# A two-layer MLP kernel: w2 loaded in four transfers of nine row tiles in place of six of six

## The chip, the cores and the metric

The kernel runs on one core of one Trainium2 chip. The metric is device time in microseconds (us) of one execution. The program uses one core, so there is no second die to compare. The kernel before takes 290.91 us (median of 3 runs, 290.85 to 291.09). A profile's span is about 1.8 us shorter than the time of the same run.

## The reference

```python
B, S, D, F = 1, 2048, 576, 4608          # all bf16
h   = einsum("bsd,df->bsf", x, w1) + b1
h   = relu(h) ** 2
out = einsum("bsf,fd->bsd", h, w2) + b2
```

w2 is 4608 x 576 in bf16: 36 row tiles of 128 rows, 5.31 MB, nearly half of the 11.36 MB that the profile counts as read from HBM (that count is the sum of all loads but the three blocks of x that are transposed on the way).

## The kernel before

The 2048 rows of x are taken in four blocks of 512. The first layer (`a_full`, `a_rows`) makes the 36 tiles of h for a block, and the second layer (`phase_t` for 128 of the 576 output columns, transposed; `phase_b` for the other 448) reduces over those 36 tiles. The order is: first layer of blocks 0 and 1, second layer of 0 and 1, then the same for blocks 2 and 3. So w2 is not needed until two first layers are done.

The w2 load and its place among the loads on the SyncE queue (SP), with cuts:

```python
    w2_sb = wpool.tile([P, NFT, D], BF16, name="w2_sb")         # NFT = 36
    w2_view = w2.rearrange("(ft p) d -> p ft d", p=P)
    W2CH = 6

    def load_w2(c):
        keep(nc.sync.dma_start(out=w2_sb[:, c * W2CH:(c + 1) * W2CH, :],
                               in_=w2_view[:, c * W2CH:(c + 1) * W2CH, :]))
    # ... cut ...
    load_xT(1)                                  # second x block, transposed by DMA
    for (j0, j1) in [(12, 14), (14, 16)]:       # the last parts of w1
        load_w1(nc.sync, 0, j0, j1)
        load_w1(nc.sync, 1, j0, j1)
    keep(nc.sync.dma_start(out=b2_bc[:], in_=b2.partition_broadcast(P)))
    for c in (0, 3, 1, 4, 2, 5):
        load_w2(c)
    load_xT(2)

    alloc_hT(0)
    a_full(0, "k_outer")
    a_rows(0, 12, 1)
    alloc_hT(1)
    load_xT(3)
    a_rows(1)
    a_full(1, "rows_first")
    phase_t(0, hTs[0])                          # the first reader of w2
    # ... cut ...
```

`phase_t` reads w2 in the order in which the first layer makes the tiles of h: 4, 20, 5, 21, 6, 22, ... 19, 35, then 0 to 3. That is why the chunks are loaded from both halves alternately.

```python
    ft_order = list(range(G))                   # G = 4, NJ = 16
    for j in range(NJ):
        ft_order += [G + j, G + NJ + j]
    t_order = ft_order[G:] + ft_order[:G]

    def phase_t(sb, hT):
        pt = ps_o.tile([P, SB], FP32, name="pt", tag="po")
        for i, ft in enumerate(t_order):
            keep(nc.tensor.matmul(pt[:], lhsT=w2_sb[:, ft, DM:D], rhs=hT[:, ft, :],
                                  start=(i == 0), stop=(i == NFT - 1)))
        # ... cut: bias, transposed store ...
```

## Time and profile before

| What | Before | Where it is read |
|---|---|---|
| time, median of the first 3 runs | 290.91 us | the runs |
| span, TensorE busy | 289.4 us, 285.2 us (99%) | the page, part 1 |
| granted TensorE clock | 1.0 | the list of cores |
| w2: issued, landed | 28.0 to 39.4 us on the queue; the last one, issued at 37.3 us, within 10.3 us | timeline of SP, the tile's own view |
| first reader of w2 | 75.7 us | the tile's own view |

The page of the kernel before. PE is TensorE; "busy" is in us with the share of the span; the DMA row is the busy share in tenths for 40 slices of 7.2 us, and the row under it what was moved in each slice. The last line is one kind of transfer: how many, the size of one, and the median time from issue to landing.

```profile
span 289.4 us, 4699 instructions
PE 285.2 (99%) x2032; PEld 138.9 (48%) x2032; DVE 78.5 (27%) x176; ACT 96.7 (33%) x154; POOL 2.3 (1%) x10
...
DMA  7999999400001100000000000000000110000000
GB/s 196 222 248 179 320 386 218 85 0 2 0 18 34 38 16 18 16 16 18 16 16 2 1 2 0 2 0 2 0 2 0 36 39 16 16 17 32 19 16 18
...
w_sb<-in_w_dram SPq DMA_DIRECT2D x6, 864.0 KB, 9.9
```

TensorE is busy throughout, while the DMA engines are nearly idle after the eighth slice. The view of waits, for TensorE (PE) alone, shows how little it stands still (us in total, times, longest):

```profile
PE wps L63 <- PEq L344: 0.8, 1, 0.8
PE pn L227 <- DMA w1n<-in_w_dram: 0.2, 1, 0.2
```

Neither of the two waits is on w2. The timeline of the SP queue (start, duration, operation) shows where w2 is issued: behind w1 and b2, ahead of the third x block.

```profile
26.99 0.94 SPq L304 DMA_DIRECT2D b_bc<-in_b_dram  x1
27.97 11.43 SPq L134 DMA_DIRECT2D w_sb<-in_w_dram  x6
39.44 7.88 SPq L126 DMA_TRANSPOSE xTw<-in_x_dram  x1
```

The stages are seen best in the chain of waits (start, duration, what). Line L270 is `phase_t`, L289 `phase_b`, L291 the addition of b2 to the last output:

```profile
76.09 15.54 PE pt L270 x72
91.63 54.48 PE po L289 x288
...
286.40 0.29 DVE o_sb L291
```

The view by windows (window, its length, then busy us of PE, PEld, DVE, ACT, POOL with the number of instructions, the granted clock, the DMA share and GB/s) shows the rate at which w2 arrives:

```profile
12.00:75.70 63.70, 63.70 (x577) 28.57 (x574) 29.85 (x70) 42.42 (x68) 0.00 (x0) 1.00 0.72 173
36.00:40.00 4.00, 4.00 (x42) 1.76 (x38) 2.23 (x6) 2.65 (x5) 0.00 (x0) 1.00 1.09 389
```

TensorE is busy 63.70 of 63.70 us up to the first use of w2, and the DMA engines move 389 GB/s while w2 is in flight. (The DMA share can come out above 1, as here.)

The slack is read from the view of the tile of w2: the first weight load that reads it (count, then min/median/max duration in ns, first and last start), its six transfers, and the time from issue to landing.

```profile
L270 PEld LDWEIGHTS <-w_sb x144: 98/98/98, 75.7 to 231.2; 128*128 128x128 bf16 x144
L134 SPq DMA_DIRECT2D w_sb<-in_w_dram x6: 1526/1873/2223, 28.0 to 37.3; - x6
DMA to landing us min/median/max: 8.3/9.9/10.3
```

The last transfer has landed by 37.3 + 10.3 = 47.6 us at the latest, about 28 us before 75.7 us.

### The profile page before, as it was taken

The numbers are of one execution on the slowest core, as the hardware profiler recorded it, in microseconds if no ns is written. First come the engines' busy times: TensorE is split into PE (matmuls) and PEld (weight loads), VectorE is DVE, ScalarE is ACT, GpSimd is POOL, SyncE is SP. The second block draws the span as 40 slices with busy tenths as digits, with TensorE's granted clock in tenths as the row PEclk, the third lists the DMA queues.
The fourth block names the chain that finished last, engine by engine and source line by source line (L and its number), as shares of the span: only waits on it lengthen the run. The fifth ranks groups of instructions, "written<-read, shape, count | busy, mean of one in ns | idle before, by whom it ended". The sixth has DMA issues, their size and how long they took to land.

```text
span 289.4 us, 4699 instructions
## 1 busy us (share of the span) xinstructions
PE 285.2 (99%) x2032; PEld 138.9 (48%) x2032; DVE 78.5 (27%) x176; ACT 96.7 (33%) x154; POOL 2.3 (1%) x10
## 2 busy tenths in 40 slices
PE   8999999999999999999999999999999999999995
PEld 4544444444444555555544444444444455555554
DVE  1644544444500200000025444444440001100001
ACT  3666666666500000000027666666770000000000
POOL 3000000000000000000000000000000000000000
PEclk9999999999999999999999999999999999999999
DMA  7999999400001100000000000000000110000000
GB/s 196 222 248 179 320 386 218 85 0 2 0 18 34 38 16 18 16 16 18 16 16 2 1 2 0 2 0 2 0 2 0 36 39 16 16 17 32 19 16 18
DMA packets 31637, 16.52 MB, mean 57 GB/s; under 512 B 15732, under 2 KB 31616, under 8 KB 31616
## 3 DMA queue, kind: packets, MB, share of 16 engines
q1 hardware_dynamic: 31264, 15.91, 22.1%
q8 instruction: 16, 0.26, 0.4%
q10 hardware_dynamic: 288, 0.30, 0.3%
q14 instruction: 5, 0.04, 0.0%
q0 software_dynamic: 64, 0.01, 0.0%
HBM read 11.36 MB, written 2.36 MB: 47 GB/s over the span
## 4 chain that ended last, share of the span: by engine, by line
PE 97%; DMA 1%; SPq 0%; DVE 0%; issue 0%
PE ph L188 42%; PE po L289 38%; PE pt L270 11%; PE pn L209 4%; DMA w1n<-in_w_dram 1%; PE pn L227 1%; PE ph L190 1%; PE pn L203 1%; SPq L75 0%; SPq L72 0%; DVE o_sb L291 0%; PE tb L149 0%; PE b1T_ps L166 0%; PE pn L205 0%
## 5 line engine op out<-in xcount | busy, mean ns | idle before, releaser
L188 PE MATMUL ph<-xTw,w_h 64*128 64x512 bf16 x576 | 124.6, 376 | 0.0
L190 PE MATMUL ph<-xTw,w_h 64*128 64x512 bf16 x576 | 124.6, 376 | 0.0
L289 PE MATMUL po<-w_sb,hT 128*128 128x448 bf16 (+2 forms) x612 | 109.4, 341 | 0.0
L176 ACT ACTIVATE r<-ph,b1T 128x512 bf16<-128x512 f32 x128 | 81.1, 685 | 41.6 <-PE ph L190 41.6
L188 PEld LDWEIGHTS <-w_h 64*128 64x128 bf16 x576 | 54.1, 94 | 68.3
L289 PEld LDWEIGHTS <-hT 128*128 128x128 bf16 x612 | 58.5, 98 | 51.0
L177 DVE TENSOR_TENSOR hT<-r 128x512 bf16<-128x512 bf16 x144 | 61.2, 425 | 75.9 <-ACT r L176 75.7
L190 PEld LDWEIGHTS <-w_h 64*128 64x128 bf16 x576 | 54.1, 94 | 0.0
L291 DVE TENSOR_TENSOR o_sb<-po,b_bc 128x448 bf16<-128x448 f32 (+2 forms) x17 | 10.2, 597 | 125.8 <-PE po L289 125.8
L270 PE MATMUL pt<-hT,w_sb 128*128 128x512 bf16 x144 | 31.4, 379 | 0.0
L176 ACT ACTIVATE r<-pn,b1T 128x512 bf16<-128x512 f32 x16 | 10.3, 688 | 61.0 <-PE pn L205 59.6
L270 PEld LDWEIGHTS <-w_sb 128*128 128x128 bf16 x144 | 14.1, 98 | 17.0
L273 ACT ACTIVATE oT<-pt,b2T 128x512 bf16<-128x512 f32 x4 | 2.7, 687 | 28.3 <-PE pt L270 28.3
L209 PE MATMUL pn<-xTw,w1n 128*128 128x512 bf16 x48 | 10.9, 379 | 0.0
L209 PEld LDWEIGHTS <-w1n 128*128 128x128 bf16 x48 | 4.5, 98 | 6.0 <-issue 0.8
L227 PE MATMUL pn<-xTw,w1n 128*128 128x256 bf16 x32 | 4.2, 273 | 0.4 <-DMA w1n<-in_w_dram 0.2
L63 PE MATMUL wps<-const-bfloat16-1.0 128*128 128x512 bf16 (+1 forms) x7 | 2.8, 581 | 0.8 <-PEq L344 0.8
L227 PEld LDWEIGHTS <-w1n 128*128 128x128 bf16 x32 | 2.9, 98 | 1.2 <-DMA w1n<-in_w_dram 0.9
L119 DVE COPY xTw<-xTw 64x2048 bf16<-64x2048 bf16 x4 | 2.8, 689 | 0.2
L120 DVE COPY xTw<-xTw 64x2048 bf16<-64x2048 bf16 x4 | 2.7, 687 | 0.1
L156 DVE COPY xTw<-tb 128x256 bf16<-128x256 bf16 x4 | 1.1, 292 | 6.2 <-PE tb L149 6.2
L203 PE MATMUL pn<-xTw,w1n 64*128 64x512 bf16 x8 | 2.4, 379 | 0.0
(23 smaller groups left out, 13.8 us busy)
## 6 DMA issues: line engine op xcount, KB each, us to landing
w_sb<-in_w_dram SPq DMA_DIRECT2D x6, 864.0 KB, 9.9
w_h<-in_w_dram SPq DMA_DIRECT2D x14, 288.0 KB, 7.2
out_dram<-o_sb SPq DMA_DIRECT2D x15, 112.0 KB, 1.7
w_h<-in_w_dram SPq DMA_DIRECT2D x4, 144.0 KB, 3.6
w1n<-in_w_dram SPq DMA_DIRECT2D x4, 128.0 KB, 3.6
out_dram<-ot SPq DMA_DIRECT2D x4, 128.0 KB, 2.0
x_sb<-in_x_dram ACTq DMA_DIRECT2D x2, 144.0 KB, 2.9
x_sb<-in_x_dram SPq DMA_DIRECT2D x2, 144.0 KB, 3.3
```

The source lines that it names most:

```text
L63: keep(nc.tensor.matmul(wps[:, 0:n], lhsT=ones[:, 0:P], rhs=ones[:, 0:n], start=True, stop=True))
L119: keep(nc.vector.tensor_copy(out=xT[0:H, SPC:SPC + 4, :], in_=xT[H:P, E3:E3 + 4, :]))
L176: keep(nc.scalar.activation(out=r[:], in_=bank[:], func=ACT.Relu, bias=b1T[:, ft:ft + 1], scale=1.0))
L177: keep(nc.vector.tensor_tensor(out=hTs[sb][:, ft, :], in0=r[:], in1=r[:], op=ALU.mult))
L188: keep(nc.tensor.matmul(bx[:], lhsT=w1_h[0:H, LO_C[i], jc], rhs=xT[0:H, LO_W[i], :], start=(i == 0), stop=(i == NC - 1)))
L190: keep(nc.tensor.matmul(by[:], lhsT=w1_h[H:P, UP_C[i], jc], rhs=xT[H:P, UP_W[i], :], start=(i == 0), stop=(i == NC - 1)))
L203: keep(nc.tensor.matmul(banks[2 * i][:], lhsT=w1n8[0:H, i, :], rhs=xT[0:H, SPC, :], start=start, stop=stop, skip_group_check=order == "k_o ...
L209: keep(nc.tensor.matmul(banks[g][:], lhsT=w1n[:, k, g * P:(g + 1) * P], rhs=xT[:, O + k, :], start=start, stop=stop))
L227: keep(nc.tensor.matmul(banks[g][:, hc], lhsT=w1n[:, k, g * P:(g + 1) * P], rhs=xT[:, O + k, hc], start=(h == 0 and k == 0), stop=False, s ...
L270: keep(nc.tensor.matmul(pt[:], lhsT=w2_sb[:, ft, DM:D], rhs=hT[:, ft, :], start=(i == 0), stop=(i == NFT - 1)))
L289: keep(nc.tensor.matmul(po[:, 0:d1 - d0], lhsT=hT[:, ft, jj * P:(jj + 1) * P], rhs=w2_sb[:, ft, d0:d1], start=(i == 0), stop=(i == NFT - 1)))
L291: keep(nc.vector.tensor_tensor(out=o_sb[:, d0:d1], in0=po[:, 0:d1 - d0], in1=b2_bc[:, d0:d1], op=ALU.add))
```

## The change

Fewer, larger transfers for w2, on the idea that each transfer has a fixed cost: four of 1,296 KB in place of six of 864 KB. The order still alternates between the halves of w2.

```diff
-    W2CH = 6
+    W2CH = 9
...
-    for c in (0, 3, 1, 4, 2, 5):
+    for c in (0, 2, 1, 3):
         load_w2(c)
```

## The prediction

> **What bounds the kernel now.** TensorE. The page gives PE busy 285.2 us of a 289.4 us span (99%), granted clock 1.0 (list of cores). The waits view finds only two waits of PE: 0.8 us before the warm-up matmuls and 0.2 us for a w1 tile. The window table gives PE 63.70 of 63.70 us between 12.0 and 75.7 us, 16.30 of 16.30 between 75.7 and 92.0, and no gap over 0.04 us up to 286.4 us. The chain of waits is 97% PE; the rest is its start (x and w1 landing) and its tail (last addition 0.29 us, last store about 1.5 us).
>
> **What the change does.** The same 5.31 MB of w2 (6 x 864 KB) goes out as 4 transfers of 1,296 KB on the same queue, still bringing both halves (tiles 0-8 and 18-26) first. The order listing shows the same rows of PE, ACT, DVE and POOL. Only semaphore lanes rotate by two, so later stores wait for other, long finished transfers, and TensorE waits for w2 four times instead of six.
>
> **Cost.** Before, the six issues took 1.5 to 2.2 us each on the SP queue (11.43 us in all, from 28.0 to 39.4), each landing 8.3 to 10.3 us after its issue. At 32 to 46 us the core moved 342 to 392 GB/s, so the stretch is bound by bytes, which don't change. The Trainium skill (DMA: Bandwidth & Descriptors, Anatomy of one DMA) gives a fixed cost of about 2 us per transfer, which would make two fewer worth at most 4 us; I don't grant that, since six transfers overlap and the bytes already flow at that rate. Estimates: issues of about 2.3 to 3.3 us, 10 to 12 us in all; landing 10 to 15 us after issue; w2 complete at 46 to 50 us, against at most 37.3 + 10.3 = 47.6 us before. The next transfer, the transpose of the third x block, starts within 1.5 us of its former 39.4 us.
>
> **How much is on the critical path: none.** The first reader of w2 is the weight load of the transposed tail phase at 75.7 us: about 28 us of slack. The first layer of blocks 0 and 1 runs in between, and needs only w1 and x. The w1 transfers and the second x block are issued before w2 (until 27 us) and keep their times. The third and fourth x blocks, issued behind w2 (39 to 52 us; traffic over by 54 us), are read only from about 91.6 us on. PE runs at full density throughout, so freed DMA time can't speed it.
>
> **Predicted time:** 290.9 us, 290.3 to 291.6 us 8 times in 10. Faster by over 2%: 1%; within 2%: 98%; slower by over 2%: 1%.
>
> **What would show each step.** Right: PE busy within 0.3 us of 285.2; phases at 75.7, 91.6, 146.1 and 216 us unmoved within 0.3 us; no wait of PE for w2 in the waits view; four w2 issues of 1,296 KB, median issue and landing 1.3 to 1.5 times as long, total issue 10 to 12 us, same GB/s at 32 to 46 us. Wrong on bytes-bound: w2 done over 3 us earlier. Wrong on slack: idle time of PE before 91.6 us beyond what it had, or a shifted start of the tail phase.
>
> **What would make it wrong.** Longer w2 bursts disturbing the last w1 or second x block landings (those queue ahead, so I doubt it); the lane rotation making a late store wait for a slow transfer (all are spaced by 6 us and land in 2); a granted clock under 1.0; or a chip-to-chip difference of a few tenths of a microsecond, which most of my range is for.

## The result, and the profile after

The changed kernel takes 291.16 us (median of 4 runs, 290.94 to 291.46), the kernel before on the same chip 291.00 us (median of 4, 290.85 to 291.09). The ratio is 1.0007 with a 95% interval of 0.999 to 1.0024: the same. Here and below a ratio is the mean time of one kernel's fast runs over that of the other's fast runs of the same rounds, so it is not quite the ratio of the medians.

The page after, the same lines:

```profile
span 289.6 us, 4693 instructions
PE 285.5 (99%) x2027; PEld 139.9 (48%) x2032; DVE 78.6 (27%) x176; ACT 96.7 (33%) x154; POOL 2.3 (1%) x10
...
DMA  7999999400001200000000000000000110000000
GB/s 198 221 245 188 308 389 212 92 0 2 0 14 25 52 16 18 16 16 18 16 16 2 1 2 0 2 0 2 0 2 0 36 38 16 16 16 19 33 16 18
...
w_sb<-in_w_dram SPq DMA_DIRECT2D x4, 1296.0 KB, 12.7
```

The waits of TensorE, the SP queue and the chain of waits after:

```profile
PE wps L63 <- PEq L344: 0.8, 1, 0.8
PE pn L209 <- issue: 0.3, 2, 0.2
PE tb L149 <- DMA x_sb<-in_x_dram: 0.2, 1, 0.2
```

```profile
26.91 0.82 SPq L304 DMA_DIRECT2D b_bc<-in_b_dram  x1
27.77 10.21 SPq L134 DMA_DIRECT2D w_sb<-in_w_dram  x4
38.03 9.78 SPq L126 DMA_TRANSPOSE xTw<-in_x_dram  x1
```

```profile
76.61 7.34 PE pt L270 x34
84.00 8.15 PE pt L270 x37
92.15 54.48 PE po L289 x288
...
286.92 0.29 DVE o_sb L291
```

The tile of w2 after:

```profile
L134 SPq DMA_DIRECT2D w_sb<-in_w_dram x4: 423/3064/3531, 27.8 to 34.7; - x4
DMA to landing us min/median/max: 9.2/12.7/13.5
```

And the same two windows after:

```profile
12.00:75.70 63.70, 63.54 (x578) 28.63 (x576) 29.87 (x70) 42.49 (x68) 0.00 (x0) 1.00 0.73 173
36.00:40.00 4.00, 4.00 (x40) 1.83 (x38) 2.54 (x6) 2.65 (x5) 0.00 (x0) 1.00 1.08 390
```

The reader should see four things. The transfers of w2 are fewer and each takes longer to land (12.7 us median in place of 9.9). The bytes flow at the same rate (390 and 389 GB/s). TensorE waits for w2 in neither kernel. And every stage of the second trace lies 0.52 us later (92.15 against 91.63, 286.92 against 286.40), while the span is only 0.2 us longer: something at the start cost half a microsecond, and something at the very end gave 0.3 us back. Both are settled below. (In the chain after, the first stage of L270 comes in two pieces because two matmul records are missing from that trace: 142 in place of 144. The 63.54 us of the first window is another such gap.)

### The profile page after: what moved, and what is told of

Its sections match the earlier page's. It is cut to its first block, busy times and chain, and to the rows that moved or that the text cites. A ratio compares the mean times of both kernels' runs of the same rounds, so it can differ in the third digit from the quotient of the medians.

```text
span 289.6 us, 4693 instructions
## 1 busy us (share of the span) xinstructions
PE 285.5 (99%) x2027; PEld 139.9 (48%) x2032; DVE 78.6 (27%) x176; ACT 96.7 (33%) x154; POOL 2.3 (1%) x10
## 4 chain that ended last, share of the span: by engine, by line
PE 98%; DMA 1%; issue 0%; DVE 0%
PE ph L188 42%; PE po L289 38%; PE pt L270 11%; PE pn L209 4%; PE pn L227 1%; DMA x_sb<-in_x_dram 1%; PE tb L149 1%; PE ph L190 1%; PE pn L203 1%; DVE o_sb L291 0%; PE b1T_ps L166 0%; PE pn L205 0%
## 5 line engine op out<-in xcount | busy, mean ns | idle before, releaser
L270 PE MATMUL pt<-hT,w_sb 128*128 128x512 bf16 x142 | 31.3, 379 | 0.1
L270 PEld LDWEIGHTS <-w_sb 128*128 128x128 bf16 x144 | 14.1, 98 | 17.0
L227 PE MATMUL pn<-xTw,w1n 128*128 128x256 bf16 x32 | 4.6, 295 | 0.0
L227 PEld LDWEIGHTS <-w1n 128*128 128x128 bf16 x32 | 3.3, 107 | 0.5
L149 PE MATMUL tb<-ident,x_sb 128*128 128x128 bf16 x20 | 2.4, 288 | 0.2 <-DMA x_sb<-in_x_dram 0.2
## 6 DMA issues: line engine op xcount, KB each, us to landing
w_sb<-in_w_dram SPq DMA_DIRECT2D x4, 1296.0 KB, 12.7
```

The source lines that it names most:

```text
L149: keep(nc.tensor.transpose(bank[:, slot, qc], xs[:, j, c0:c0 + P], ident[:]))
L227: keep(nc.tensor.matmul(banks[g][:, hc], lhsT=w1n[:, k, g * P:(g + 1) * P], rhs=xT[:, O + k, hc], start=(h == 0 and k == 0), stop=False, s ...
```

## The experiments

The theory: w2 is off the path, because its last byte lands about 28 us before its first reader; while it is in flight the bytes bind, not the number of transfers. The rivals: each transfer has a cost that shows (the 2 us that the prediction quotes from the Trainium skill); the slack is not there or the traffic disturbs other stages; and, for the 0.52 us, that the change itself moved the stages.

Kernels are compared only within the same rounds. All outputs are right.

| Kernel | w2 load | Time, median us | Before, median us | Ratio, 95% interval |
|---|---|---|---|---|
| mid6 | 6 x 6, held to about 59 us | 291.28 | 291.29 | 1.0009 (0.9994 to 1.0023) |
| mid9 | 4 x 9, held to about 59 us | 291.34 | 291.29 | 1.0003 (0.9986 to 1.002) |
| late6 | 6 x 6, held to about 74 us | 301.45 | 291.29 | 1.0354 (1.0338 to 1.0369) |
| late9 | 4 x 9, held to about 74 us | 303.06 | 291.29 | 1.041 (1.0395 to 1.0426) |
| two18 | 2 x 18, old place | 290.94 | 291.43 | 0.9989 (0.9976 to 1.0001) |
| many36 | 36 x 1, old place | 290.72 | 291.43 | 0.9983 (0.997 to 0.9995) |
| before_again | 6 x 6, old place | 291.25 | 291.43 | 0.9997 (0.9983 to 1.0011) |
| after_again | 4 x 9, old place | 291.15 | 291.43 | 0.999 (0.9978 to 1.0003) |
| late3 | 12 x 3, held to about 74 us | 301.49 | 291.25 | 1.0341 (1.0322 to 1.0359) |
| late1 | 36 x 1, held to about 74 us | 304.17 | 291.25 | 1.0443 (1.0429 to 1.0457) |
| edge9 | 4 x 9, held to about 66.5 us | 297.82 | 291.25 | 1.0214 (1.0192 to 1.0236) |
| many36_again | 36 x 1, old place | 290.99 | 291.25 | 0.9988 (0.9975 to 1) |

Against a threshold of 2%, late6, late9, late3 and late1 are slower, edge9 is unclear (it is slower than before, but its interval holds 1.02), and all others are the same.

### Is the slack real? mid6 and mid9

To use up the slack without removing a wait, the w2 transfers are put behind a small transfer that reads a tile of h of block 1. The SP queue is in order, so w2 is issued only when that tile has been made (in mid9 the small transfer is issued at 58.63 us, w2 from 59.24 us). The argument is the row tile j at which this happens. The edit has a side effect: the third and fourth x blocks no longer stand behind w2, and go out earlier (from 29.68 us in mid9, 39.44 us before). It also adds eight lines, so that `phase_t` is L278 in these traces.

```diff
+    gate = const.tile([P, 64], BF16, name="gate")
+    def gated_w2(sb, j):
+        keep(nc.sync.dma_start(out=gate[:], in_=hTs[sb][:, G + NJ + j, 0:64]))
+        for c in (0, 2, 1, 3):                 # (0, 3, 1, 4, 2, 5) with W2CH = 6
+            load_w2(c)
...
             evac_h(sb, by, G + NJ + j)
+            if j == w2_at:
+                gated_w2(sb, j)
...
-    for c in (0, 3, 1, 4, 2, 5):
-        load_w2(c)
     load_xT(2)
...
-    a_rows(1)
+    a_rows(1, w2_at=7)
```

> The hold is on row tile 7 of block 1 (58.3 us): w2 is issued about 30 us later than in before, in six transfers. Theory (about 28 us of slack): landing complete near 75 us, no wait of TensorE on w2, time 291.0 us within 0.6. Rival (there is no such slack, or w2 traffic in another stretch disturbs the compute): slower by 1 us or more.

> The same hold in four transfers of nine. Theory: the first pair lands near 67.6 us and the last near 75 us, before its first reader (75.7 and 78.7 us); time 291.0 us within 0.6, the same as mid6. Rival: slower than mid6 by 1 us or more.

Both came out as the theory said: 291.28 and 291.34 us against 291.29 before, with no wait of TensorE on w2. In the trace of mid9 the last transfer is issued at 63.4 us and lands within 13.2 us, so by 76.6 us, 28 to 29 us later than in the changed kernel (48.2 us) and the kernel before (47.6 us).

```profile
L134 SPq DMA_DIRECT2D w_sb<-in_w_dram x4: 589/1716/3304, 59.2 to 63.4; - x4
DMA to landing us min/median/max: 6.4/11.0/13.2
76.38 15.54 PE pt L278 x72
```

The slack is real, and the traffic does not disturb the compute of another stretch either.

### What is the grain worth when w2 is late? late6 and late9

The grain is the size of one transfer. The same edit with `w2_at=15`, the last row tile. Now w2 can't arrive in time.

> w2 is held back until the last row tile of block 1 in the first layer is squared (73.9 us in the trace of before), then loaded in six transfers of six. Theory (bytes and slack: a transfer's size matters only once w2 is late): issue from about 74.4 us, last landing about 16 us later (5.31 MB at 390 GB/s is 13.6 us, and 2 us), near 90.4 us; the last chunk pair's second half is first read at the 21st of 36 matmuls, so 16 matmuls (3.4 us) follow it; TensorE loses about 10 us, time about 301 us (299 to 304). Rival (cost per transfer of 2 us that shows when exposed): six transfers lose about 4 us more than the four of late9.

> The same hold, four transfers of nine. Theory: last landing the same as late6 within 1 us, but the last chunk is first read at the 15th of 36 matmuls, so 22 matmuls (4.7 us) follow it, and the first pair lands some 2 us later: 1.3 us slower than late6, about 302.4 us. Rival (cost per transfer): about 4 us faster than late6. If both are within 0.5 us, neither grain nor count matters even when exposed.

The times were 301.45 and 303.06 us. The `phase_t` matmuls in the timeline of late6 (in brackets the idle time of TensorE before them and what ended it):

```profile
79.53 0.39 PE L278 MATMUL pt<-hT,w_sb 128*128 128x512 bf16 x1 [3.34 <-DMA w_sb<-in_w_dram]
81.84 1.46 PE L278 MATMUL pt<-hT,w_sb 128*128 128x512 bf16 x3 [1.92 <-DMA w_sb<-in_w_dram]
84.10 5.77 PE L278 MATMUL pt<-hT,w_sb 128*128 128x512 bf16 x17 [0.79 <-DMA w_sb<-in_w_dram]
90.83 11.18 PE L278 MATMUL pt<-hT,w_sb 128*128 128x512 bf16 x51 [0.97 <-DMA w_sb<-in_w_dram]
```

and of late9:

```profile
80.81 0.61 PE L278 MATMUL pt<-hT,w_sb 128*128 128x512 bf16 x1 [5.06 <-DMA w_sb<-in_w_dram]
84.24 5.97 PE L278 MATMUL pt<-hT,w_sb 128*128 128x512 bf16 x14 [2.82 <-DMA w_sb<-in_w_dram]
90.98 12.48 PE L278 MATMUL pt<-hT,w_sb 128*128 128x512 bf16 x57 [0.77 <-DMA w_sb<-in_w_dram]
```

Four transfers are slower than six here, not faster. The rival of a fixed cost per transfer, which wanted late9 to be 4 us faster, falls. The last transfer landed within 0.6 us of the same delay after the hold ended (late6: from 73.97 to 80.55 + 10.24 = 90.79 us, so 16.82 us; late9: from 73.52 to 78.47 + 12.46 = 90.93 us, so 17.41 us; the last issues and their landings are read from the chains of waits). But with four transfers the last one holds a tile that is read as the 16th of 36, with six as the 22nd (the expectations above count one too few in both, which leaves the difference as it is): 51 matmuls of 72 of the two blocks' stage were left in late6 and 57 in late9. Six matmuls of 0.2155 us (15.54 / 72 = 0.216 in the chain before) are 1.29 us; with the 0.59 us of landing, 1.88 us. Measured from the first matmul of `a_rows` (9.86 and 9.41 us), the start of `phase_b` is at 92.16 us (102.02 - 9.86) and 94.04 us (103.45 - 9.41): 1.88 us apart. Why the four landed 0.59 us later than the six is not shown.

### Is finer always better when late? late3 and late1

> The hold of late6 and late9, with twelve transfers of three row tiles. Theory (when w2 is late, the loss is set by the last landing plus the matmuls that may only follow it): bytes still flow at 390 GB/s, last landing near 90.8 us as in late6, but its tiles are first read at the 27th of 36 matmuls, so 45 of the stage's 72 matmuls remain after it in place of late6's 51: 1.3 us faster than late6, about 300.2 us (299.3 to 301). Rival (cost per transfer shows when exposed): slower than late6.

> The same hold with 36 transfers of one row tile. Theory: small transfers slow the bytes to the 260 to 283 GB/s that the trace of the 36-transfer kernel showed at 32 to 48 us, so the last landing comes near 74.5 + 20 + 2 = 96.5 us, and 41 of 72 matmuls (8.8 us) follow: about 4.5 us slower than late6, some 306 us (304 to 308). So both too coarse and too fine lose when exposed. Rival (finer is always better when exposed): faster than late3.

late1 took 304.17 us, near the low end of what was expected, because its 36 transfers moved only 294 to 324 GB/s from 80 to 94 us. late3 was a miss: 301.49 us (300.53 to 302.39), not faster than late6. In its trace, the slowest of its four runs, the last wait was on another transfer than I had counted on: not on the last one, which is first read by the 28th matmul, but on the second last (tiles 15 to 17), read by the 23rd. It landed at 91.88 us (84.10 + 7.78 in its chain), 17.65 us after the hold ended at 74.23 us, 0.8 us later than the last one of late6. So 50 matmuls remained, nearly as many as in late6, and they began later. The time in the held position is flat between three and six row tiles, and worse on both sides: too coarse leaves work behind the last landing, too fine slows the bytes.

### Where the slack ends: edge9

> The hold on row tile 11 of block 1 (squared at 66.1 us) with four transfers of nine. Theory: last landing 17.4 us after the hold ends as in late9, at 83.6 us; its first reader would run at about 79.0 us (76.1 us and 14 matmuls of 0.2155 us), so the loss is about 4.6 us and the time about 295.7 us (294.5 to 297), most of the wait in front of the 15th matmul of the stage. Rival (slack is larger than the trace says): 291 us.

The main wait is where the theory puts it, but the time was a miss: the loss was 6.6 us (297.82 - 291.25), not 4.6. The timeline of TensorE in `phase_t`, and two windows of the same trace (of PE alone: window, its length, busy us, granted clock, DMA share, GB/s):

```profile
77.52 2.12 PE L278 MATMUL pt<-hT,w_sb 128*128 128x512 bf16 x9 [0.77 <-DMA w_sb<-in_w_dram]
80.92 1.25 PE L278 MATMUL pt<-hT,w_sb 128*128 128x512 bf16 x5 [1.28 <-DMA w_sb<-in_w_dram]
84.27 14.16 PE L278 MATMUL pt<-hT,w_sb 128*128 128x512 bf16 x57 [2.10 <-DMA w_sb<-in_w_dram]
```

```profile
82.00:84.00 2.00, 0.17 (x1) 1.00 0.54 192
86.00:88.00 2.00, 2.00 (x6) 0.50 0.00 0
```

The waits come before the 2nd, the 11th and the 16th matmul (again one more than I had counted). Two parts make up 6.35 us of the loss. In the chain of the kernel before, the 16th matmul starts at 76.09 + 15 x 0.2158 = 79.33 us; here it is 0.45 us later from the start on (10.22 against 9.77 us for the first `ph` matmul, which is the first of `a_rows`), so 79.78 us without a wait, and it started at 84.27 us: 4.49 us, as the theory had it. Then, from this matmul to the start of `phase_b`, the chain has 14.16 us here (98.43 - 84.27) and 12.30 us before (91.63 - 79.33): another 1.86 us, lost after all data had landed. After 4.15 us of waits within 8 us, the granted clock fell to 0.50 and the matmuls ran at half pace. In slices of 1 us it reads 0.53 from 85 to 86 us and 0.77 from 88 to 89 us, with 0.50 between them and 1.00 around: some 3.4 us at half pace, which is 1.7 us lost. (The clock also fell to 0.50 in late6 and late9, between 80 and 90 us, but was back at 1.00 before the last landing. TensorE had to wait for that landing anyway, so there the fall cost little: the 51 matmuls after it in late6 took 0.219 us each.) One of the four runs, 296.33 us, had a mean granted clock of 0.999, the other three (297.75 to 297.97 us) 0.994: the fall of the clock is worth 1.4 to 1.9 us, and by the mean clock it does not happen in every run. The Trainium skill (TensorE: Matmul & The Clock Gate, What's actually happening) says that an idle stretch of about 3.4 us returns the array to half clock, on a window that runs freely. This trace agrees with the half clock (0.50), and the runs agree that it varies from run to run. It differs in the length of the stretch: the waits here were shorter than 3.4 us each (2.10 us the longest), with matmuls between them, and the clock fell all the same.

### Count alone, at the old place: two18 and many36

```diff
-    W2CH = 6
+    W2CH = 18                                  # many36: 1
...
-    for c in (0, 3, 1, 4, 2, 5):
+    for c in (0, 1):                           # many36: 0, 18, 1, 19, ...
```

> w2 in two transfers of 18 row tiles, at the old place. Theory (bytes bound, off the path): same GB/s at 32 to 46 us, w2 complete at 46 to 50 us, no wait of TensorE, time 291.0 us within 0.5. Rival (cost per transfer of 2 us): w2 complete some 8 us earlier than with six.

> w2 in 36 transfers of one row tile (144 KB each), at the old place. Theory: bytes bound, but the queue's issue time may now bind: 36 issues at 0.4 us or more are 14 to 30 us, w2 complete between 46 and 62 us; the third and fourth x blocks come later by as much, still before 91 us; time 291.0 us within 0.5. Rival (cost per transfer of 2 us, in series): 60 us more for w2, which would end past 100 us, TensorE waits, time over 305 us.

> The 36-transfer kernel at the old place, repeated, since its first timing came out 0.17% faster than before with an interval that just excluded 1, though its profile showed the same body. Theory (that was drift between runs of this size; the body is the same): ratio within 0.998 to 1.002, interval containing 1 or nearly. Rival (it is really faster by some 0.5 us): ratio again near 0.998 with a similar interval, and a profile with an earlier first ph matmul or a shorter tail.

From 2 to 36 transfers the time stays within 0.2% of before. The SP queue and a window of many36 show that its transfers were really slower: 20.87 us of issue in place of 11.43, and 258 GB/s in place of 389.

```profile
27.93 20.87 SPq L134 DMA_DIRECT2D w_sb<-in_w_dram  x36
```

```profile
36.00:40.00 4.00, 4.00 (x40) 1.80 (x38) 2.51 (x6) 2.65 (x5) 0.00 (x0) 1.00 0.92 258
```

With two, w2 had landed by 29.7 + 17.8 = 47.5 us, as with six (47.6 us). The saving of 2 us per transfer, which the Trainium skill (DMA: Bandwidth & Descriptors, Anatomy of one DMA) gives as the fixed cost of one transfer by the GpSimd path, is not seen in this in-order queue on SP: the transfers overlap, and four fewer of them bring w2 in 0.1 us earlier. (The page's figure is for transfers issued from GpSimd, which the prediction left out.) Why the 36 transfers are slower was not tested by a run of its own, but a later trace, that of late1, points to the time of the issues: there each of the 36 took 0.43 us (0.59 us the longest) with about 0.04 us between two, the queue waited for nothing, and 5.31 MB in the 17.19 us of these issues are 309 GB/s, which is near what was measured (294 to 324 GB/s). Nor do the runs tell bytes from rows: every grouping moves the same rows of 1,152 B (576 values of 2 B), so "the bytes bind" may as well mean that the rows do. many36 was 0.17% and then 0.12% below before, the second interval touching 1. The next section shows where about 0.3 us of this comes from: the rival of many36_again was right in part, since its trace does have a shorter tail and an earlier first `ph` matmul.

### The half microsecond at the start and the 0.3 us at the end: before_again and after_again

Both kernels were run and profiled again, unchanged.

> The kernel before, unchanged, profiled a second time. Theory (the 0.5 us by which the phases of the changed kernel's trace lie later comes from the first 10 us, where x lands and the TensorE pace rises, and varies from run to run in any kernel): first matmul of the row-tile stage (the first of ph) starts anywhere between 9.7 and 10.4 us, and all later phases follow that start with a fixed distance (145.85 us from there to the third stage's first load is not moved by over 0.1 us). Rival (the change caused the 0.5 us): 9.8 us here, 10.3 us in the changed kernel's repeat.

> The changed kernel, unchanged, profiled a second time. Theory: its first ph matmul starts anywhere between 9.7 and 10.4 us, times spread 290.9 to 291.5 us like those of before. Rival (the change caused it): 10.3 us again, with before at 9.8.

(The distance of 145.85 us in this text was a slip; the one that matters is given below.) The first `ph` matmul came at 9.87 us in before_again and at 10.01 us in after_again, against 9.77 and 10.29 us in the first two traces. So the 0.52 us is not the change's: it is decided before 10 us, when w2 has not been issued. The table shows all nine traces in which w2 is in time; the second column is read from the timeline, the third from the chain of waits.

| Trace | first `ph` matmul, us | start of last addition, us | difference | span, us | span minus last addition | lane of the last store |
|---|---|---|---|---|---|---|
| before | 9.77 | 286.40 | 276.63 | 289.4 | 3.00 | 1 |
| before_again | 9.87 | 286.49 | 276.62 | 289.5 | 3.01 | 1 |
| after | 10.29 | 286.92 | 276.63 | 289.6 | 2.68 | 7 |
| after_again | 10.01 | 286.63 | 276.62 | 289.3 | 2.67 | 7 |
| mid6 | 9.89 | 286.51 | 276.62 | 289.5 | 2.99 | 2 |
| mid9 | 10.06 | 286.69 | 276.63 | 289.6 | 2.91 | 0 |
| two18 | 9.71 | 286.33 | 276.62 | 289.1 | 2.77 | 5 |
| many36 | 10.26 | 286.89 | 276.63 | 289.6 | 2.71 | 7 |
| many36_again | 9.47 | 286.09 | 276.62 | 288.8 | 2.71 | 7 |

The body is 276.62 or 276.63 us in every one of them, whatever the transfers of w2 look like. What varies is the start (9.47 to 10.29 us, also for one and the same kernel: 9.47 and 10.26 for the 36 transfers) and the end. In the start TensorE is less dense: it waits for x or w1, and the four first matmuls of L227 take 0.60 us in the first trace of before and 1.01 us in that of after. That looks like the warm-up of the array's clock, which the Trainium skill (TensorE: Matmul & The Clock Gate, What's actually happening) calls variable from run to run; but the granted clock reads 1.00 over these first 12 us in both traces, and the cause of the start's spread stays open.

The end does depend on the change. The listing of the built program puts the transfers on eight semaphore lanes in turn, and the last store's lane follows from the number of transfers ahead of it (last column):

```
before:  L292 DMACopy out_dram<-o_sb 128x128 [waits DMAHW1_49,DVE_49]
after:   L292 DMACopy out_dram<-o_sb 128x128 [waits DMAHW7_49,DVE_49]
```

Here the number after DMAHW is the lane: a store waits for the former user of the lane that it takes. After the last store, the SP engine waits for the lanes one after the other: in the listing of every kernel here first for 1 and 2, then for 0 and 3, then for 4, 5, 6 and 7. The SP engine's semaphore waits in the 0.8 us from 0.5 us after the start of the last addition, in before (count, then min/median/max duration in ns):

```profile
L355 SPq EVENT_SEMAPHORE  x1: 1100/1100/1100, 287.1 to 287.1; - x1
```

and in after:

```profile
L355 SPq EVENT_SEMAPHORE  x5: 28/28/28, 287.6 to 287.9; - x5
```

Before, SP meets the lane of the last store first, sits in that wait for 1,100 ns, and only then goes through five more short waits. After, it goes through five short waits of 28 ns while the store is still on its way, and only then waits for it. Together with what lies between two such waits, that is the 0.3 us: in the view of waits of the SP queue the final wait is

```profile
SPq L355 <- DMA out_dram<-o_sb: 1.1, 1, 1.1
```

before (and the same in before_again), and

```profile
SPq L355 <- DMA out_dram<-o_sb: 0.8, 1, 0.8
```

after (and the same in after_again and in both traces with 36 transfers). All nine traces agree (spans are known to 0.1 us), and the tail gets shorter with the place of the lane in that order: 2.99 to 3.01 us for lanes 1 and 2, 2.91 us for lane 0, 2.77 us for lane 5, 2.67 to 2.71 us for lane 7. The five traces with a late w2 fit too: 3.01 us in late6 (lane 2), 2.88 to 2.93 us in late9, late3, late1 and edge9 (lane 0). No kernel was run that turns the lanes and does nothing else, so this is shown by the records of the waits and by the agreement of fourteen traces, and not by an edit of its own.

## Why the prediction was right

The time was 291.16 us, with 290.9 us predicted (290.3 to 291.6).

- **What bounds the kernel (right).** TensorE was busy 285.5 us after, 285.2 us before, and waited for w2 in neither.
- **Off the critical path (right, and tested).** Delaying w2 by 28 us cost nothing (mid6, mid9); delaying it beyond that cost 6 to 13 us (edge9, late6, late9, late1). The slack that the trace gave, about 28 us to the first reader, was if anything small, since the last chunk is not read by the first matmul.
- **Bytes bind, not the count (right).** The rate at 36 to 40 us was 390 GB/s after and 389 before; issues took 10.21 us in all (10 to 12 predicted). The last issue was at 34.7 us, landing at 34.7 + 13.5 = 48.2 us at most (46 to 50 predicted). The median issue grew from 1.87 to 3.06 us, 1.64 times, a little over the 1.3 to 1.5 that I gave; the median landing grew 1.28 times, a little under. Single issues were spread more widely than the 2.3 to 3.3 us that I gave: from 0.42 to 3.53 us.
- **Stages unmoved within 0.3 us (wrong in the letter).** They lay 0.52 us later in the first trace. The step that failed is that I took the first 10 us of the kernel before as fixed: they vary from 9.47 to 10.29 us over nine traces. The distances behind it are the same to 0.01 us.
- **Lanes (half right).** I named the turning of the lanes, and expected no effect. It saves 0.3 us (0.1%) at the end, by the order of the last waits, which no stage count shows and which the spread at the start hides in a single comparison.

## What to carry to other kernels

Before regrouping a transfer, find its last landing and its first reader: here 28 us lie between them, and no grain from 2 to 36 transfers moves the time by more than 0.2%. Where a load is exposed, its cost is the last landing plus the work that may only follow it, so look at which consumer reads the last chunk; larger chunks made that worse (late9 lost 1.6 us to late6), and very small ones slowed the bytes (late1 lost 2.7 us). A stall of TensorE can cost more than its own length, as the 1.4 to 1.9 us of half clock after the waits of edge9 show.

## What the Trainium skill lacked or had wrong

- DMA: Bandwidth & Descriptors gives a fixed cost of about 2 us per transfer, fitted for transfers issued from GpSimd. It does not say how little of it is left when large transfers queue behind one another on SP: here six, four and two transfers of the same 5.31 MB were complete at 47.6, 48.2 and 47.5 us at most.
- No page tells how transfer size sets the rate of a stream of queued transfers on SP. Here 144 KB each gave 258 to 283 GB/s (32 to 48 us of many36) and 294 to 324 GB/s (80 to 94 us of late1), and 864 KB or more 371 to 390 GB/s (32 to 44 us of the other traces).
- TensorE: Matmul & The Clock Gate speaks of one idle window of about 3.4 us; of shorter idle stretches it says, for another kernel, only that frequent small ones make the clock swing, without their lengths. In edge9 three waits of 0.77, 1.28 and 2.10 us, with matmuls between them, were followed by a granted clock of 0.50; by the mean clock this happened in three runs of four.
- None of the pages read mentions the waits at a program's end on the semaphore lanes of its transfers: 28 ns each here, and 0.3 us between the best and the worst place of the last store's lane.
